# Sigmoid gates and SiLU by a hyperbolic tangent, and a bias added on VectorE, in an mLSTM and two-MLP kernel

## The chip, the cores and the metric

One core of one Trainium2 chip. The time is microseconds of device time of one launch; lower is better. Several runs of a kernel are taken and the median is compared. One execution was profiled: the trace and its page are of that one.

## What is computed

An mLSTM (matrix memory with exponential gates) over 2 sequences of 768 steps with 8 heads of width 40, then two MLPs of 320 to 2048 to 320 on its 1536 output rows, the first with SiLU, the second with Mish. All in fp32:

```
m_new = max(f[t] + m, i[t])
C = exp(f[t] + m - m_new) * C + exp(i[t] - m_new) * outer(v[t], k[t]);  n likewise with k[t]
y[t] = sigmoid(o[t]) * (C q[t]) / max(|n q[t]|, 1)
h = x @ w_in;  g = h * sigmoid(h)          (layer 1: SiLU)
out = g @ w_out                            (layer 2: g = h * tanh(softplus(h)))
```

## The kernel before, in words

**Attention.** The 768 steps are cut into 6 chunks of 128 (`attention(c)`, with both sequences of a chunk together). Inside a chunk the recurrence is written as a product: scores k.q (L748) times a weight tile e (L757, into `pt`), times v (L762, into `a`), plus the state carried from the chunk before (L781, from chunk 1 on). The tile e of 128x512 holds the exponentials for four heads side by side; a chunk has four such tiles (u = 0 to 3). In chunks 0 and 1 the exponent is spread by TensorE into PSUM (L692, L694, tile `fp`), and ScalarE takes four exponentials of 128x128, one a head, since each head has its own bias per partition, a column of `bT` (L704). In chunks 2 to 5 the exponent comes by DMA and is masked by GpSimd (L717), then exponentiated in place (L730, also one head at a time).

**Gates.** The output gates of a chunk are loaded into `y1[c]`, 128x640, and `sigm` takes their sigmoid in place (L649): chunks 0 and 1 behind the last exponential of chunk 0's attention, chunks 2 to 5 behind that of chunk 2. Then GpSimd divides them by the denominator (L816), and VectorE multiplies them into the attention's output x (L819). x is transposed on TensorE (L897) and split into a high part `xh` (L907) and a low part `xl` (L910).

**Weights.** Each weight block f (16 per layer) arrives as 64-bit floats (`wr`, three buffers), is turned into fp32 by two ScalarE passes (L471, L463) and one VectorE join (L477), and split into `wh` (ScalarE, L503) and `wl` (GpSimd, L497; VectorE, L501). A buffer of `wr` is free for the next load once its join is done. All loads are issued from SP's queue, in one order.

**MLP.** A block of the first GEMM makes a PSUM tile h of 128x512 (two weight blocks by 256 rows of x, L930, 16 matmuls). ScalarE takes Silu into `g` (L964), GpSimd rounds g to `gh` (L955), VectorE forms `gl` = g - gh (L957), and the second GEMM (L947 to L949) multiplies both parts with the output weights; it runs two blocks behind the first. For chunks 0 and 1 the first layer is run in two halves (five block pairs, then three), and `store_y` keeps the first half's sum in y (`first`, L983) and adds the second half's (`more`, L987); other chunks use `first` alone. Layer 2 uses Mish (L973, L974).

**What sets the order.** Nothing is written in the order in which it runs. Every operation is handed to a planner with its engine, an estimated cost in us, the tiles that it reads and writes, and the name of the activation table that it needs. The planner simulates the engines, adds 1.28 us on ScalarE where the table changes and prefers not to change it, improves the order by 1500 random draws with a fixed seed, and then emits each engine's instructions in the order found. A changed cost, engine or table name so gives a new order for all engines. Each engine runs its own list in order. Up to 20 matmuls on a dummy tile (L445) fill TensorE while it has nothing else at the start.

Of the kernel before, what the change touches and what calls it, by code (L numbers as in the profile page):

```python
# [13 lines left out]
AF = mybir.ActivationFunctionType  # L14
ALU = mybir.AluOpType
# [23 lines left out]
class Plan:  # L39
# [13 lines left out]
    def buf(self, pool, shape, dtype, tag, bufs=1, name=None):  # L53
        b = Buf(pool, shape, dtype, tag, bufs, name or tag)
        ring = self.rings.setdefault((id(pool), tag), [])
        b.before = ring[-bufs] if len(ring) >= bufs else None
        b.prev = ring[-1] if ring else None
        ring.append(b)
        return b
# [310 lines left out]
def kernel(  # L370
# [17 lines left out]
    DM = out.shape[1]  # L388
# [10 lines left out]
    op, buf = plan.op, plan.buf  # L399
    pe, act, dve, pool = nc.tensor, nc.scalar, nc.vector, nc.gpsimd  # L400
# [21 lines left out]
    def mk4():  # L422
        return mk.t.unsqueeze(1).to_broadcast([128, 4, 128])
# [102 lines left out]
    bT = buf(sb, [128, NCH, 16], F32, "bT")  # L526
# [112 lines left out]
    last_e = [None]  # L639
# [3 lines left out]
    y1 = [buf(sb, [128, B, DM], F32, f"y{c}") for c in range(NCH)]  # L643
# [2 lines left out]
    last = NCH - 1  # L646

    def sigm(c, after):
        return op("ACT", 0.74, lambda: act.activation(out=y1[c].t, in_=y1[c].t, func=AF.Sigmoid),  # L649
           w=[y1[c]], table="sig", after=after)  # L650

    def load_o(c, after=()):
        dma(y1[c], None, lambda: y1[c].t, lambda: og[c], 128 * B * DM * 4, after=after)
# [1 line left out]
    def attention(c):  # L655
        A = "attn"
        hurry = HURRY0 if c == 0 else HURRY
        g0 = gate_of[c]

        kq = buf(sb, [104, 2048], F32, "kq")  # L660
        for e in range(2):
            r = slice(64 * e, 64 * e + D)
# [17 lines left out]
        for u in range(4):  # L680

            if c >= PEBC and ((c - PEBC) * 4 + u) % 7 < 3:
                e = buf(sb, [128, 512], F32, "ga", bufs=3)
            else:
                e = buf(sb, [128, 512], F32, "e", bufs=EB)
            es.append(e)
            if c < PEBC:

                fp = buf(ps, [128, 512], F32, ("h", "h", "o0", "h")[u], bufs=(2, 2, 1, 2)[u])

                def spread(u=u, fp=fp):
                    pe.matmul(out=fp.t, lhsT=idb.t, rhs=mk4(), start=True, stop=False)  # L692
                    for i in range(4):
                        pe.matmul(  # L694
                            out=fp.t[:, i * 128:(i + 1) * 128],
                            lhsT=ct.t[:, u * 4 + i:u * 4 + i + 1].to_broadcast([128, 128]),
                            rhs=gc.t[:, c * 128:(c + 1) * 128], start=False, stop=(i == 3),
                        )

                def weight(u=u, e=e, fp=fp):  # L700
                    for i in range(4):
                        k = slice(i * 128, (i + 1) * 128)
                        j = u * 4 + i
                        act.activation(out=e.t[:, k], in_=fp.t[:, k], func=AF.Exp, bias=bT.t[:, c, j:j + 1])  # L704

                op("PE", 1.09, spread, r=[idb, mk, ct, (gc, c)], w=[fp], hurry=hurry, duty=0.59)
                last_e[0] = op("ACT", 1.14, weight, r=[(bT, g0), fp], w=[e], table="exp", hurry=hurry,
                               after=sig if c == 0 else ())
                continue

            def row(u=u):
                return gd.t[4 * u:4 * u + 4, :].rearrange("h t -> (h t)").unsqueeze(0).to_broadcast([128, 512])


            def cut(e=e):
                ev = e.t.rearrange("p (h t) -> p h t", h=4)
                pool.affine_select(  # L717
                    out=ev, in_=ev, pattern=[[0, 4], [1, 128]], base=0, channel_multiplier=-1,
                    compare_op=ALU.is_ge, fill=-1e30,
                )  # L720

            dma(e, gd, lambda e=e: e.t, row, 128 * 2048, hurry=hurry)
            op("POOL", 0.59, cut, w=[e], hurry=hurry, grain=0.7)
# [8 lines left out]
        for us in EXPS[c] if c >= PEBC else []:  # L732
            last_e[0] = op("ACT", 1.28 * len(us), lambda us=us: exps(us), r=[(bT, g0)], w=[es[u] for u in us],
                           table="exp", hurry=hurry)
        for i in SIGS.get(c, ()):
            sigm(i, [last_e[0]])
        xs = []
        for b in range(2):
# [12 lines left out]
            for hf in range(2):  # L751
                u = 2 * b + hf
# [49 lines left out]
            else:  # L802
# [3 lines left out]
               r=[nsrc], w=[dn], hurry=hurry)  # L806
# [153 lines left out]
    def silu(hp):  # L960
        g = buf(sb, [128, 512], F32, "g", bufs=2)
        gh = buf(sb, [128, 512], F32R, "gh", bufs=3)
        gl = buf(sb, [128, 512], F32R, "gl", bufs=3)
        op("ACT", 0.6, lambda: act.activation(out=g.t, in_=hp.t, func=AF.Silu), r=[hp], w=[g], table="silu")  # L964
        parts(g, gh, gl)
        return gh, gl

# [11 lines left out]
    def store_y(c, b, po, part):  # L979
        y = y1[c]  # L980

        def first():
            act.copy(out=y.t[:, b, :], in_=po.t[:, 0:DM])  # L983


        def more():
            dve.tensor_tensor(out=y.t[:, b, :], in0=y.t[:, b, :], in1=po.t[:, 0:DM], op=ALU.add)  # L987

        if part == 2:
            op("DVE", 0.49, more, r=[po], w=[(y, b)])  # L990
        else:
            op("ACT", 0.43, first, r=[po], w=[(y, b)])
# [42 lines left out]
    sig = [sigm(c, ()) for c in SIGS.get(-1, ())]  # L1035
# [173 lines left out]
```

## Time and profile before

| | |
|---|---|
| median of 3 runs | 450.71 us (449.8 to 451.85) |
| profiled execution | span 447.9 us from the first to the last instruction; no other time of it is shown |
| mean granted TensorE clock | 0.973 of full speed (2.4 GHz) |
| busy: TensorE, VectorE, ScalarE, GpSimd | 435.0, 196.2, 249.4, 145.1 us |
| ScalarE table loads | 34, of 1.28 us each |

A busy share is of the whole span. PE is TensorE's matmuls and PEld its weight loads, which run beside them; DVE is VectorE, ACT ScalarE, POOL GpSimd, SP the queue from which transfers are issued. L964 is line 964 of the kernel. An engine's idle time matters only where that engine, or one that waits for it, sets the end.

### The profile page before, as it was taken

Reading aid. Unit: us, or ns where it says so; the run is one execution under the profiler, and the core shown is the slowest. Engines: PE = TensorE matmul, PEld = TensorE weight load, DVE = VectorE, ACT = ScalarE, POOL = GpSimd, SP = SyncE. Lnnn points to the kernel's source line nnn. Section 1 sums busy time; section 2 is a strip of 40 time slices with the busy share of each in tenths; the row PEclk is TensorE's granted clock in tenths of the full one; section 3 lists DMA queues with packets and bytes.
Section 4 is the critical chain, followed back from the end, with each engine's and each line's share of the span. In section 5 each row is a group of like instructions: output and inputs, shape, how many; then the busy total and the mean of one; then the engine's idle time right before and its main releaser. Section 6 shows DMA issues by size and latency. Waiting matters only on the chain.

```text
span 447.9 us, 8297 instructions
## 1 busy us (share of the span) xinstructions
PE 435.0 (97%) x3366; PEld 424.6 (95%) x3366; DVE 196.2 (44%) x340; ACT 249.4 (56%) x441; POOL 145.1 (32%) x208
## 2 busy tenths in 40 slices
PE   7978989999999999999999999999999999999997
PEld 4858889999999999999999999999999999999996
DVE  4486587644774555664442644322131221221111
ACT  1898667799989888873124447433343333333331
POOL 1777686862361434122113996300000000000000
PEclk9956969999999999999999999999999999999999
DMA  7869979152475767865000453100000000000000
GB/s 223 301 225 268 324 241 318 67 166 71 112 249 185 291 213 277 279 205 201 3 1 1 131 156 103 34 31 0 2 31 0 1 31 0 31 1 0 31 2 29
DMA packets 16785, 54.18 MB, mean 121 GB/s; under 512 B 2003, under 2 KB 3731, under 8 KB 16267
## 3 DMA queue, kind: packets, MB, share of 16 engines
q1 hardware_dynamic: 16747, 53.65, 36.5%
q8 instruction: 26, 0.43, 0.4%
q14 instruction: 12, 0.10, 0.1%
HBM read 45.88 MB, written 7.77 MB: 120 GB/s over the span
## 4 chain that ended last, share of the span: by engine, by line
PE 89%; POOL 4%; ACT 3%; DMA 2%; issue 1%; DVE 1%; POOLq 0%; ACTq 0%
PE h L930 29%; PE o L947 12%; PE o L949 12%; PE o L948 12%; PE s L930 10%; PE a L762 4%; PE s L748 2%; POOL wl L497 2%; PE a L897 2%; DMA wr<-w 2%; PE o L445 1%; PE a L781 1%; PE a L846 1%; ACT e L704 1%; PE h L694 1%
## 5 line engine op out<-in xcount | busy, mean ns | idle before, releaser
L947 PE MATMUL o<-wh,gh 128*128 128x320 f32 x384 | 121.1, 315 | 0.0
L949 PE MATMUL o<-wh,gl 128*128 128x320 f32 x384 | 119.1, 310 | 0.4 <-DVE gl L957 0.4
L948 PE MATMUL o<-wl,gh 128*128 128x320 f32 x384 | 118.4, 308 | 0.0
L930 PE MATMUL h<-xh,wh 128*128 128x256 f32 x432 | 111.0, 286 | 0.0
L930 PE MATMUL h<-xl,wh 128*128 128x256 f32 x432 | 109.0, 281 | 0.0
L975 DVE TENSOR_TENSOR gl<-e,gh 128x512 fp32r<-128x512 f32 x48 | 33.8, 703 | 126.6 <-ACT e L974 126.6
L930 PEld LDWEIGHTS h<-xh,wh 128*128 128x128 f32 x432 | 82.5, 191 | 0.6 <-issue 0.2
L930 PEld LDWEIGHTS h<-xl,wh 128*128 128x128 f32 x432 | 82.3, 190 | 0.0
L949 PEld LDWEIGHTS o<-wh,gl 128*128 128x128 f32 x384 | 72.1, 188 | 0.7 <-DVE gl L957 0.7
L947 PEld LDWEIGHTS o<-wh,gh 128*128 128x128 f32 x384 | 72.3, 188 | 0.5
L948 PEld LDWEIGHTS o<-wl,gh 128*128 128x128 f32 x384 | 72.3, 188 | 0.0
L497 POOL TENSOR_TENSOR wl<-wt,wh 128x192 fp32r<-128x192 f32 x96 | 64.7, 704 | 15.9 <-ACT wh L503 13.4
L957 DVE TENSOR_TENSOR gl<-g,gh 128x512 fp32r<-128x512 f32 x48 | 40.6, 851 | 43.9 <-POOL gh L955 43.7
L930 PE MATMUL h<-xh,wl 128*128 128x256 f32 x288 | 58.0, 283 | 0.0
L955 POOL TENSOR_SCALAR gh<-g 128x512 fp32r<-128x512 f32 x48 | 32.3, 674 | 77.2 <-ACT g L964 74.9
L964 ACT ACTIVATE g<-h 128x512 f32<-128x512 f32 x48 | 28.5, 598 | 41.4 <-PE h L930 40.9
L930 PEld LDWEIGHTS h<-xh,wl 128*128 128x128 f32 x288 | 44.3, 190 | 0.0
L973 ACT ACTIVATE gh<-h 128x512 fp32r<-128x512 f32 x24 | 14.5, 602 | 50.5 <-PE h L930 50.4
L973 ACT ACTIVATE gh<-s 128x512 fp32r<-128x512 f32 x24 | 14.4, 601 | 49.5 <-PE s L930 49.5
L930 PE MATMUL s<-xh,wh 128*128 128x256 f32 x144 | 36.4, 282 | 0.0
L930 PE MATMUL s<-xl,wh 128*128 128x256 f32 x144 | 36.0, 279 | 0.0
L477 DVE SCALAR_TENSOR_TENSOR wt<-wt,wr 128x704 int32<-128x704 int32 x32 | 31.8, 997 | 5.7 <-ACT wt L463 5.1
(101 smaller groups left out, 621.0 us busy)
## 6 DMA issues: line engine op xcount, KB each, us to landing
wr<-w SPq DMA_DIRECT2D x32, 704.0 KB, 6.4
wd<-wt SPq DMA_DIRECT2D x16, 352.0 KB, 5.3
wt<-wd SPq DMA_DIRECT2D x16, 352.0 KB, 3.1
vk<-vk SPq DMA_DIRECT2D x6, 729.0 KB, 4.0
kq<-qk SPq DMA_DIRECT2D x12, 320.0 KB
e<-gd SPq DMA_DIRECT2D x8, 256.0 KB, 5.9
ga<-gd SPq DMA_DIRECT2D x8, 256.0 KB, 3.3
y<-og SPq DMA_DIRECT2D x6, 320.0 KB, 11.3
```

What stands on the lines that cost most here:

```text
L477: dve.scalar_tensor_tensor(out=ti, in0=ti, scalar=3, in1=r.t[:, :, 0], op0=ALU.logical_shift_left, op1=ALU.bitwise_or)
L497: pool.tensor_tensor(out=wl.t[:, k], in0=t.t[:, k], in1=wh.t[:, k].bitcast(F32), op=ALU.subtract)
L762: pe.matmul(out=pa.t[:, h * V:(h + 1) * V], lhsT=pt.t[:, i * 128:(i + 1) * 128], rhs=vb.t[:, b, h * V:(h + 1) * V], start=True, stop=True,)
L930: pe.matmul(out=hp.t[:, f % 2 * 256:(f % 2 + 1) * 256], lhsT=w.t[:, k], rhs=xx.t[:, i, :], start=(n == 0), stop=(n == len(terms) - 1),)
L947: pe.matmul(out=o, lhsT=gh.t[:, ts], rhs=wh.t[:, O], start=(first and f == 0), stop=False)
L948: pe.matmul(out=o, lhsT=gh.t[:, ts], rhs=wl.t[:, O], start=False, stop=False)
L949: pe.matmul(out=o, lhsT=gl.t[:, ts], rhs=wh.t[:, O], start=False, stop=(end and f == 1))
L955: op("POOL", 0.63, lambda: pool.tensor_scalar(out=gh.t, in0=g.t, scalar1=1.0, scalar2=1.0, op0=ALU.mult, op1=ALU.mult), r=[g], w=[gh])
L957: op("DVE", 0.75, lambda: dve.tensor_tensor(out=gl.t, in0=g.t, in1=gh.t.bitcast(F32), op=ALU.subtract), r=[g, gh], w=[gl], grain=1.0)
L964: op("ACT", 0.6, lambda: act.activation(out=g.t, in_=hp.t, func=AF.Silu), r=[hp], w=[g], table="silu")
L973: op("ACT", 0.6, lambda: act.activation(out=gh.t, in_=hp.t, func=AF.Mish), r=[hp], w=[gh], table="mish")
L975: op("DVE", 0.7, lambda: dve.tensor_tensor(out=gl.t, in0=g.t, in1=gh.t.bitcast(F32), op=ALU.subtract), r=[g, gh], w=[gl])
```

## The change

The gates' sigmoid becomes tanh(o/2) on ScalarE and 0.5 z + 0.5 on GpSimd, in place. SiLU becomes tanh(h/2) on ScalarE and (z + 1) h on VectorE, which is twice SiLU; the factor of two is taken out where the first layer's output is copied or added to y (times 0.5). Both tanh are named to the planner as needing the exponential's table. In chunks 0 and 1 VectorE adds the bias of four heads to the spread exponents, from PSUM into e, and ScalarE takes one exponential of 128x512 in place.

```diff
--- before.py
+++ after.py
@@ -646,8 +646,11 @@
     last = NCH - 1
 
     def sigm(c, after):
-        return op("ACT", 0.74, lambda: act.activation(out=y1[c].t, in_=y1[c].t, func=AF.Sigmoid),
-           w=[y1[c]], table="sig", after=after)
+        o = op("ACT", 0.74, lambda: act.activation(out=y1[c].t, in_=y1[c].t, func=AF.Tanh, scale=0.5),
+           w=[y1[c]], table="exp", after=after)
+        op("POOL", 0.85, lambda: pool.tensor_scalar(
+            out=y1[c].t, in0=y1[c].t, scalar1=0.5, scalar2=0.5, op0=ALU.mult, op1=ALU.add), w=[y1[c]])
+        return o
 
     def load_o(c, after=()):
         dma(y1[c], None, lambda: y1[c].t, lambda: og[c], 128 * B * DM * 4, after=after)
@@ -697,15 +700,16 @@
                             rhs=gc.t[:, c * 128:(c + 1) * 128], start=False, stop=(i == 3),
                         )
 
-                def weight(u=u, e=e, fp=fp):
-                    for i in range(4):
-                        k = slice(i * 128, (i + 1) * 128)
-                        j = u * 4 + i
-                        act.activation(out=e.t[:, k], in_=fp.t[:, k], func=AF.Exp, bias=bT.t[:, c, j:j + 1])
+                def shift(u=u, e=e, fp=fp):
+                    dve.tensor_tensor(
+                        out=e.t.rearrange("p (h t) -> p h t", h=4), in0=fp.t.rearrange("p (h t) -> p h t", h=4),
+                        in1=bT.t[:, c, 4 * u:4 * u + 4].unsqueeze(2).to_broadcast([128, 4, 128]), op=ALU.add,
+                    )
 
                 op("PE", 1.09, spread, r=[idb, mk, ct, (gc, c)], w=[fp], hurry=hurry, duty=0.59)
-                last_e[0] = op("ACT", 1.14, weight, r=[(bT, g0), fp], w=[e], table="exp", hurry=hurry,
-                               after=sig if c == 0 else ())
+                op("DVE", 0.7, shift, r=[(bT, g0), fp], w=[e], hurry=hurry)
+                last_e[0] = op("ACT", 0.6, lambda e=e: act.activation(out=e.t, in_=e.t, func=AF.Exp),
+                               w=[e], table="exp", hurry=hurry, after=sig if c == 0 else ())
                 continue
 
             def row(u=u):
@@ -961,7 +965,9 @@
         g = buf(sb, [128, 512], F32, "g", bufs=2)
         gh = buf(sb, [128, 512], F32R, "gh", bufs=3)
         gl = buf(sb, [128, 512], F32R, "gl", bufs=3)
-        op("ACT", 0.6, lambda: act.activation(out=g.t, in_=hp.t, func=AF.Silu), r=[hp], w=[g], table="silu")
+        op("ACT", 0.6, lambda: act.activation(out=g.t, in_=hp.t, func=AF.Tanh, scale=0.5), r=[hp], w=[g], table="exp")
+        op("DVE", 0.7, lambda: dve.scalar_tensor_tensor(
+            out=g.t, in0=g.t, scalar=1.0, in1=hp.t, op0=ALU.add, op1=ALU.mult), r=[hp], w=[g])
         parts(g, gh, gl)
         return gh, gl
 
@@ -980,11 +986,13 @@
         y = y1[c]
 
         def first():
-            act.copy(out=y.t[:, b, :], in_=po.t[:, 0:DM])
+            act.mul(out=y.t[:, b, :], in_=po.t[:, 0:DM], mul=0.5)
 
 
         def more():
-            dve.tensor_tensor(out=y.t[:, b, :], in0=y.t[:, b, :], in1=po.t[:, 0:DM], op=ALU.add)
+            dve.scalar_tensor_tensor(
+                out=y.t[:, b, :], in0=po.t[:, 0:DM], scalar=0.5, in1=y.t[:, b, :], op0=ALU.mult, op1=ALU.add
+            )
 
         if part == 2:
             op("DVE", 0.49, more, r=[po], w=[(y, b)])
```

## Rows read from the trace of the kernel before

**Rows 1.** The page's first part: busy us (share of the span) and instructions by engine
```profile
PE 435.0 (97%) x3366; PEld 424.6 (95%) x3366; DVE 196.2 (44%) x340; ACT 249.4 (56%) x441; POOL 145.1 (32%) x208
```

**Rows 2.** Stretches of the span: length, each engine's busy us (instructions), clock, DMA
```profile
core 0: us, PE busy (x) PEld busy (x) DVE busy (x) ACT busy (x) POOL busy (x), PEclk, DMA share, GB/s
22.50:24.00 1.50, 0.26 (x3) 0.14 (x2) 0.31 (x1) 1.50 (x3) 0.88 (x2) 0.98 0.16 30
24.00:36.00 12.00, 8.97 (x43) 7.37 (x44) 11.09 (x21) 11.11 (x24) 7.31 (x11) 0.50 0.72 242
...
36.00:41.00 5.00, 5.00 (x31) 4.55 (x30) 4.31 (x7) 4.54 (x7) 4.68 (x6) 0.50 0.96 268
41.00:52.00 11.00, 10.57 (x81) 10.31 (x81) 5.49 (x8) 8.91 (x13) 8.85 (x13) 1.00 1.01 317
...
120.00:130.00 10.00, 10.00 (x91) 9.68 (x90) 8.70 (x13) 8.30 (x12) 6.24 (x7) 1.00 0.62 188
...
300.00:440.00 140.00, 140.00 (x1082) 139.95 (x1081) 30.44 (x50) 47.53 (x93) 0.00 (x0) 1.00 0.04 13
```

**Rows 3.** The chain that ended last: start us, us, what
```profile
17.73 1.28 ACT L649
...
19.77 1.28 ACT L704
21.06 1.14 ACT e L704 x4
22.20 0.73 ACT wr L471
...
24.50 0.69 DVE pt L757
...
131.99 1.89 PE h L930 x16
135.63 1.89 PE h L930 x16
```

**Rows 4.** Timeline of TensorE around 23 us: start, us, what [idle before it]
```profile
20.89 1.88 PE L762 MATMUL a<-vk,pt 128*128 128x41 f32 x16
25.23 3.64 PE L762 MATMUL a<-vk,pt 128*128 128x41 f32 x16 [2.47 <-DVE pt L757]
```

**Rows 5.** Timeline of ScalarE, VectorE and SP's queue before 43 us
```profile
16.57 1.14 ACT L704 ACTIVATE e<-h,bT 128x128 f32<-128x128 f32 x4
...
23.69 0.89 DVE L477 SCALAR_TENSOR_TENSOR wt<-wt,wr 128x704 int32<-128x704 int32 x1 [3.08 <-ACT wt L463]
...
24.61 4.10 SPq L403 DMA_DIRECT2D wr<-w  x3
...
39.63 1.28 ACT L649 ACT_TABLE_LOAD   x1
...
41.68 1.28 ACT L964 ACT_TABLE_LOAD   x1
```

**Rows 6.** Waits of TensorE: who waited for whom, us in total, times, longest
```profile
PE o L949 <- DVE gl L957: 0.4, 1, 0.4
```

**Rows 7.** Instruction groups (ScalarE within 70 to 266 us): busy, mean ns | idle before
```profile
L964 ACT ACTIVATE g<-h 128x512 f32<-128x512 f32 x44 | 26.1, 598 | 39.0 <-PE h L930 38.6
L964 ACT ACT_TABLE_LOAD x14 | 18.0, 1283 | 3.4 <-PE h L930 3.2
...
L730 ACT ACT_TABLE_LOAD x10 | 12.8, 1283 | 0.2
...
L649 ACT ACT_TABLE_LOAD x4 | 5.1, 1283 | 0.1
...
L955 POOL TENSOR_SCALAR gh<-g 128x512 fp32r<-128x512 f32 x48 | 32.3, 674 | 77.2 <-ACT g L964 74.9 <-DVE xl L910 2.3
...
L555 POOL TENSOR_SCALAR ga<-ga 80x512 f32<-80x512 f32 x1 | 1.5, 1492 | 0.1
```

**Rows 8.** Two lines of VectorE: duration ns min/median/max, first and last start us
```profile
L957 DVE TENSOR_TENSOR gl<-g,gh x48: 676/693/1203, 44.7 to 262.7; 128x512 fp32r<-128x512 f32 x48
...
L757 DVE TENSOR_TENSOR pt<-e,s x16: 677/681/689, 14.3 to 210.4; 128x512 f32<-128x512 f32 x16
```

## The prediction

> **What bounds the kernel now.** I read the page's busy shares first, to see which engine to follow: TensorE is busy for 97% of the 447.9 us span, ScalarE for 56%, VectorE for 44%, GpSimd for 32% [rows 1]. An average over unlike stages says little, so I cut the span into stretches. From 70 us to 440 us TensorE is never idle at a granted clock of 1.00; the stretches 120 to 130 and 300 to 440 stand for all of them [rows 2]. There ScalarE cannot be what sets the end. Before 70 us it is different: TensorE works 0.26 of 1.5 us, then 8.97 of 12, and its granted clock is 0.50 from 24 to 41 us, 1.2 GHz instead of 2.4 [rows 2]. So the question is only what the change does to the first 70 us, and whether it spoils the full stretch behind them.
>
> The chain of waits names the cause of the first hole. ScalarE loads the sigmoid table at 17.73, gates one tile, loads the exponential's table again at 19.77, does four exponentials, and only then, from 22.20, turns to the first weight block [rows 3]. VectorE's join of that block starts at 23.69 after 3.08 us of waiting for ScalarE, and the product pt, which needs nothing of the weights, stands behind it in VectorE's order and starts at 24.50 [rows 3, 5]. TensorE had finished the previous group of 16 products at 20.89 + 1.88 = 22.77 and starts the next at 25.23: a hole of 2.46 us. In front of the hole 16 matmuls took 1.88 us, behind it 16 of the same took 3.64, since the clock had fallen [rows 4]. Everything of chunk 0, its outputs x and the first GEMM, follows behind that.
>
> **The change, part by part.**
> *Table loads.* 28 loads, 18.0 + 12.8 + 5.1 = 35.9 us of ScalarE, lie between 70 and 266 us [rows 7]. They lie beside a TensorE that is full: worth 0. Four count: the two at 17.73 and 19.77, and the two around the second gate tile at 39.63 and 41.68, each 1.28 us [rows 3, 5].
> *Exponentials of chunks 0 and 1.* Four of 128x128 cost 1.14 us of the engine (the chain's row at 21.06); one over 512 columns should cost what the other 512-column activation costs, 0.60 us [rows 3, 7]. Two such groups, at 16.57 and 21.06, stand ahead of the first weight block [rows 3, 5]: 2 x 0.54 = 1.08. VectorE gets eight additions that read PSUM and write 512 columns; nearest row pt, 0.68 us [rows 8], 5.4 us in all. From 20.6 to 23.69 VectorE only waits, so I cost those that fall there at 0; without that cover each costs 0.68 (rival below). One group's latency grows by 0.68 + 0.60 - 1.14 = 0.14 us, hidden by TensorE's products before it.
> *First hole.* ScalarE reaches the weights 2 x 1.28 + 1.08 = 3.6 us earlier, so the join is over before pt can start. pt then waits only for its buffer, which the products from 20.89 release, so I expect the 2.46 us hole closed. If TensorE does not pause there, the next group also runs at the full clock: 3.64 - 1.88 = 1.76. Sum 4.2 us for chunk 0's chain. The weights move too: SP issues the next weight loads at 24.61, right behind the join [rows 5], and these issues come up to 3.6 us earlier. The DMA engines can carry that: unused share 0.84 x 1.5 + 0.28 x 12 = 4.6 us before 36 us [rows 2]. From 36 to 52 us they are full (0.96 and 1.01), so what lands there moves by no more than 3.6. Bounds of this term: 0 (the hole opens elsewhere) to 4.2; I take **3.6**, because the full DMA stretch is nearest to what decides the time up to 52 us.
> *Second pair of loads.* Without them the first SiLU tile starts up to 2 x 1.28 = 2.57 us earlier. TensorE's wait for that tile's low part gl is 0.4 us in all [rows 6]: **0.4**, bounds 0 and 2.57.
> *SiLU in two steps.* Tanh costs what Silu did (0.60), and VectorE adds 48 passes over a PSUM tile at 0.68, 32.6 us in all. For the first tile the pass is hidden by the 2.57 just freed. From 70 us on each tile has cover: the second GEMM runs two blocks behind, and a block lasts 135.63 - 131.99 = 3.64 us of TensorE [rows 3], against 0.68. The tightest stretch is 120 to 130 us, VectorE busy 8.70 of 10 [rows 2]; two or three more passes fill it. If that cover is gone, three late tiles cost 3 x 0.68 = 2.0. I take 0 and keep 2.0 for the range.
> *Gates.* Six GpSimd passes over 640 columns. The nearest row, the same form with two constants over 512, is 0.67, so 0.67 x 640/512 = 0.84; the other row, one constant over 80x512, is 1.49, so at most 1.9 [rows 7]. I take 0.84. Behind such a pass stand the weights' low parts and the key scaling in GpSimd's order, and VectorE's x waits for them through the gate. One falls before 36 us, where GpSimd is busy 7.31 of 12 [rows 2]: 0. The second tile's gate is not needed until chunk 1, so 0; placed ahead of SiLU's rounding in the backlog of 36 to 41 us (4.68 of 5) it costs 0.84 to 1.9.
> *Halving at the first layer's end* replaces instructions one for one, with the same operands: 0. No DMA is added or moved past another by hand; the planner draws its whole order anew, whose effect no row bounds other than the ends below.
> Contention: gl, with two SBUF inputs, varies from 676 to 1203 ns; pt, with one input in PSUM, stays within 677 to 689 [rows 8]. The new VectorE passes are like pt, hence 0.68. The Trainium skill ("GPSIMD Engine Reference", section Specifications) says that GpSimd shares its SBUF interfaces with VectorE and collides with VectorE instructions that have two SBUF inputs. The rows on gl and pt agree; by that rule the two early gate passes could stretch a join or gl by 1203 - 676 = 527 ns each, and the sum would be about 1.1 us smaller, 447.8.
>
> **Sum.** 3.6 + 0.4 = 4.0 us off a span of 447.9 gives 443.9. The median of the runs shown, 450.7, lies 2.8 above that span; the profiled execution has no other time shown, so I leave the 2.8 as it is: **446.7 us**.
>
> **Rivals.**
> *A, the forecast* (443 to 448.4).
> *B, hidden anyway.* The hole closes but chunk 1's input waits for the same transfers, so TensorE starves later instead. For it: DMA share 0.96 and 1.01 from 36 to 52 us. Against: the unused 4.6 us before. Only the 0.4 is left: 450.3.
> *C, VectorE becomes the bound of the start.* It is busy 11.09 of 12 us from 24 to 36 and 4.31 of 5 behind [rows 2]. If the four additions of chunk 1 stand there, among joins and pt, they put back the chain they were to free: 4 x 0.68 = 2.7, with nothing gained, 453.4 us. It decides once more than the free time, 0.91 + 1.19 (VectorE works 0.31 of the 1.5 us ahead) = 2.1 us, has to be found there, that is from the fourth addition on. Against: ScalarE freed early pulls the joins out of this stretch.
> *D, the clock does not fall.* If the closed hole keeps TensorE at 2.4 GHz through 24 to 41 us, its 8.97 + 5.00 us of work there shrink by half, 7.0, of which 1.76 is counted: 446.7 - 5.2 = 441.5. Against: it also pauses for the transposes, 3 of 12 us.
> *E, the change does not do what it says.* If Tanh is not in the exponential's table the loads stay, and the first SiLU tile pays 0.68 and chunk 1 the 0.14: 451.5. The trace before runs no Tanh and cannot tell. The Trainium skill ("ScalarE: Activation LUTs", section on table sets) lists tanh as a member of exp_and_others; no run here shows it.
>
> **How the numbers follow.** About 0.5% (2.25 us) is what a measurement of this kernel can tell from no change. A 0.47 and D 0.13 are faster: 0.60. B 0.20 and E 0.03 are within: 0.23. C is slower: 0.17. The likeliest is A: 446.7. The low end is D's 441.5 less 0.5 of the 0.4's upper bound, 441.0; the high end is C's 453.4. Outside lie a D that also gains behind 52 us, and a C with the late tiles' 2.0 on top: 0.2 together.
>
> **What would show it.** Right: one table load before the SiLU stage and one for Mish; four rows of 512-column exponentials per chunk at 0.60; the additions at 0.68; no hole near 22.8 us; the first weight issues behind the first three at about 21; TensorE full from about 66 us. Wrong: VectorE idle less than 0.9 us between 22 and 36 with pt waiting for its queue (C); the same wait moved to a DMA of vk or wr (B); TensorE idle behind 70 us, released by gl (the cover of the late tiles is gone).

## The result, and the profile after

The changed kernel takes **452.94 us** (median of 20 runs, 452.06 to 453.70); the kernel before took 450.07 beside it (20 runs, 447.55 to 454.48). The ratio is 1.0063, 95% interval 1.0046 to 1.0080: 0.6% slower. The forecast was 446.7, faster. The value lies inside the range, but on the side of the chance of 0.17.

The profiled execution has a span of 451.4 us, against 447.9 before, and a time of 453.1, so 1.7 us lie around the span. (The forecast added 2.8. The other 1.1 would mean that the execution profiled before was quicker than its median.) 3.5 us of span have to be found.

First the page's row of busy time by engine.

```profile
PE 435.3 (96%) x3366; PEld 424.1 (94%) x3366; DVE 229.9 (51%) x396; ACT 204.9 (45%) x385; POOL 153.5 (34%) x214
```

Then the groups of instructions that the change made or left (line, engine, operation, tiles, count; busy us, mean ns of one; idle time before them and what ended it):

```profile
L968 ACT ACTIVATE g<-h 128x512 f32<-128x512 f32 x48 | 28.7, 597 | 55.5 <-PE h L934 52.2 <-DVE gl L961 3.2
...
L711 ACT ACTIVATE e<-e 128x512 f32<-128x512 f32 x8 | 4.8, 626 | 1.9 <-DVE e L704 1.9
L607 ACT ACT_TABLE_LOAD x1 | 1.3, 1283 | 0.8 <-PEq L1207 0.8
L979 ACT ACT_TABLE_LOAD x1 | 1.3, 1283 | 0.0
...
L969 DVE SCALAR_TENSOR_TENSOR g<-g,h 128x512 f32<-128x512 f32 x48 | 32.8, 684 | 26.8 <-ACT g L968 26.5
...
L704 DVE TENSOR_TENSOR e<-h,bT 128x512 f32<-128x512 f32 x6 | 4.0, 681 | 1.0 <-PE h L697 1.0
...
L651 POOL TENSOR_SCALAR y<-y 128x640 f32<-128x640 f32 x6 | 5.6, 925 | 4.3 <-ACT y L649 4.2
```

The change does what it says [rows 1, 7]. Of 34 table loads two are left, ScalarE works 44.5 us less, VectorE 33.7 us more, GpSimd 8.4 more, and TensorE's busy time is the same. One exponential over 512 columns took 0.626 us, SiLU's tanh 0.597, the addition 0.681, the SiLU pass 0.684, the gate pass 0.925 on average.

Now the start. This is the timeline of after from 20 to 38 us, all engines (start us, us, engine, line, what, and in brackets the idle time before it and who ended it); it answers to [rows 3 to 5].

```profile
20.91 0.74 ACT L649 ACTIVATE y<-y 128x640 f32<-128x640 f32 x1 [3.11 <-DMA y<-og]
...
22.60 0.83 ACT L471 ACTIVATE wr<-wr 128x704 int32<-128x704 uint16 x1
...
24.18 1.82 DVE L477 SCALAR_TENSOR_TENSOR wt<-wt,wr 128x704 int32<-128x704 int32 x1 [4.17 <-ACT wt L463]
25.92 0.68 DVE L761 TENSOR_TENSOR pt<-e,s 128x512 f32<-128x512 f32 x1
...
26.65 3.60 PE L766 MATMUL a<-vk,pt 128*128 128x41 f32 x16 [3.44 <-DVE pt L761]
...
28.48 7.01 POOL L497 TENSOR_TENSOR wl<-wt,wh 128x192 fp32r<-128x192 f32 x9
35.46 0.71 POOL L820 TENSOR_TENSOR y<-y,dn 128x320 f32<-128x320 f32 x1
...
36.20 0.49 DVE L823 TENSOR_TENSOR x<-a,y 128x320 f32<-128x320 f32 x1 [2.81 <-POOL y L820]
...
36.84 0.66 PE L901 MATMUL a<-ct,x 128*128 128x128 f32 x2 [3.74 <-DVE x L823]
```

Read it from the top. The table loads in front of the first weight block are gone, and ScalarE still reaches that block (L471) only at 22.60; it was 22.20 before [rows 3]. It sits idle for 3.11 us in front of the tanh of the *second* gate tile, whose transfer, issued at 7.27 us, has not landed. The whole old chain then follows: join at 24.18, pt behind it, and TensorE's hole is 3.44 us instead of 2.47 [rows 4]. The join adds to it: it takes 1.82 us, where the one before took 0.89 [rows 5], beside two GpSimd passes (at 23.97 and, the gate pass of the second tile, at 25.33). A second wait is new: GpSimd makes nine low parts of weights, 7.01 us, before it divides a gate by the denominator, so x is late and TensorE waits 3.74 us. The chain that ended last has that transfer as one of its longest pieces (start us, us, what):

```profile
7.27 13.62 DMA y<-og
```

The waits of TensorE repeat those for x and pt (3.7 and 3.4 us) and show two smaller ones (who waited for whom, us in total, times, longest):

```profile
PE o L953 <- DVE gl L961: 1.0, 3, 0.6
...
PE o L951 <- POOL gh L959: 0.6, 1, 0.6
```

Last, stretches of after (length; busy us and instructions of TensorE's matmuls, its weight loads, VectorE, ScalarE, GpSimd; granted clock, DMA):

```profile
0.00:75.00 75.00, 62.92 (x451) 54.58 (x452) 54.75 (x106) 40.71 (x66) 48.06 (x69) 0.89 0.78 254
...
24.00:36.00 12.00, 6.40 (x35) 5.55 (x35) 8.71 (x16) 9.66 (x16) 10.70 (x14) 0.63 0.70 228
...
27.00:45.00 18.00, 13.54 (x71) 12.11 (x71) 14.40 (x29) 13.20 (x22) 14.39 (x19) 0.53 0.83 281
...
58.00:65.00 7.00, 6.71 (x62) 6.20 (x60) 6.80 (x13) 3.20 (x5) 6.95 (x10) 1.00 0.67 202
...
95.00:100.00 5.00, 4.21 (x30) 3.86 (x30) 3.82 (x7) 3.25 (x10) 5.00 (x8) 1.00 0.63 247
...
300.00:440.00 140.00, 140.00 (x1073) 139.95 (x1072) 30.23 (x50) 48.02 (x93) 0.00 (x0) 1.00 0.04 13
```

and three of these stretches in the kernel before:

```profile
0.00:75.00 75.00, 65.35 (x447) 57.40 (x448) 49.68 (x98) 53.03 (x98) 48.23 (x71) 0.84 0.83 269
...
58.00:65.00 7.00, 7.00 (x43) 6.78 (x40) 5.37 (x13) 3.79 (x7) 6.24 (x9) 0.51 0.70 225
...
95.00:100.00 5.00, 5.00 (x50) 4.76 (x50) 1.16 (x2) 4.95 (x10) 1.63 (x4) 1.00 0.29 68
```

Three things stand there (the row of 24 to 36 us is for a rival, below; the rows of 0 to 75 us are read after the next table). The clock falls once more in the start, for about as long as before (0.53 over 18 us), but a second fall, at 58 to 65 us in the kernel before, is gone: 62 matmuls instead of 43 in those 7 us. At 95 to 100 us TensorE is idle for 0.79 us, where it was never idle. And in the last 140 us, with TensorE busy for all of them at clock 1.00 in both kernels, it finished **1073 matmuls instead of 1082** [rows 2].

That last line can't be seen in a busy share, so I made an account by work done. For each stretch I took its length less the matmuls that start in it, each at the spacing that its form has in the full stretch of the kernel before (0.118 us in the first GEMM, 0.147 in the second, and so on). The work so priced is 410.8 us in every kernel here; what is left over is lost time:

| lost us in | 0–75 | 75–110 | 110–200 | 200–266 | 266–300 | 300–440 | rest | sum |
|---|---|---|---|---|---|---|---|---|
| before | 29.7 | 0.5 | 1.9 | 0.8 | 0.3 | 0.4 | 3.5 | 37.1 |
| after | 29.1 | 1.7 | 2.7 | 1.6 | 0.4 | 1.6 | 3.5 | 40.6 |

So of the 3.5 us, the start gave back 0.6 where about 4 was forecast, 1.2 was lost at 75 to 110 us, and 2.9 behind 110 us, in stretches where TensorE looks full in both.

The 0.6 is the difference of two larger things. TensorE is idle for 12.08 of the first 75 us in after and for 9.65 before: the waits cost 2.4 us more. Against that, the mean granted clock of these 75 us is 0.89 instead of 0.84, because the second fall did not come. That fall cost the kernel before about 3.4 us (an estimate from its row: TensorE busy for all of the 7.00 us at 0.51, so about half of them lost). Without this gain the start would have come out about 2.8 us slower than before.

### The profile page after: what moved, and what is told of

Same layout as the page of the kernel before. It is cut to its first block, busy times and chain, and to the rows that moved or that the text cites. A ratio compares the mean times of both kernels' runs of the same rounds, so it can differ in the third digit from the quotient of the medians.

```text
span 451.4 us, 8352 instructions
## 1 busy us (share of the span) xinstructions
PE 435.3 (96%) x3366; PEld 424.1 (94%) x3366; DVE 229.9 (51%) x396; ACT 204.9 (45%) x385; POOL 153.5 (34%) x214
## 4 chain that ended last, share of the span: by engine, by line
PE 80%; POOL 8%; DMA 4%; DVE 2%; issue 2%; ACT 2%; SPq 0%; POOLq 0%; ACTq 0%
PE h L934 26%; PE o L951 12%; PE o L953 11%; PE o L952 11%; PE s L934 10%; POOL wl L497 6%; PE a L766 3%; DMA y<-og 3%; PE s L752 2%; PE a L901 2%; PE a L785 1%; DMA ga<-gf 1%; PE a L850 1%; POOL gh L959 1%; DVE gl L961 1%
## 5 line engine op out<-in xcount | busy, mean ns | idle before, releaser
L934 PE MATMUL h<-xh,wh 128*128 128x256 f32 x432 | 112.6, 289 | 0.0
L934 PE MATMUL h<-xl,wh 128*128 128x256 f32 x432 | 110.9, 286 | 0.7 <-DVE xl L914 0.7
L959 POOL TENSOR_SCALAR gh<-g 128x512 fp32r<-128x512 f32 x48 | 33.9, 708 | 71.2 <-DVE g L969 62.1
L969 DVE SCALAR_TENSOR_TENSOR g<-g,h 128x512 f32<-128x512 f32 x48 | 32.8, 684 | 26.8 <-ACT g L968 26.5
```

Source lines behind the costliest of these rows:

```text
L934: pe.matmul(out=hp.t[:, f % 2 * 256:(f % 2 + 1) * 256], lhsT=w.t[:, k], rhs=xx.t[:, i, :], start=(n == 0), stop=(n == len(terms) - 1),)
L959: op("POOL", 0.63, lambda: pool.tensor_scalar(out=gh.t, in0=g.t, scalar1=1.0, scalar2=1.0, op0=ALU.mult, op1=ALU.mult), r=[g], w=[gh])
L969: op("DVE", 0.7, lambda: dve.scalar_tensor_tensor(out=g.t, in0=g.t, scalar=1.0, in1=hp.t, op0=ALU.add, op1=ALU.mult), r=[hp], w=[g])
```

## The experiments

Two theories stood at first: that the change is a gain in itself and the planner's new order gives it back, and that the passes added on VectorE and GpSimd cost the time in any order. A third came up for the last 140 us: that the tiles' places in SBUF slow the matmuls. Medians of the kernel before differ between the chips that the runs were taken on (449.66 to 451.21 us), so across chips I compare ratios to the kernel before and the account of lost time, not medians. Added lines shift the line numbers of each experiment by a few.

### The change in the order of the kernel before

To take the planner out, the order that it found for the kernel before was written down and used as a list, with the added operations put in where they fall due. q1 has the whole change, q2 the tanh half alone, q3 the bias half alone.

```diff
     def issue(self):
+        for n in ORDER:
+            self.ops[n].fn()
+        self.ops = []
+        return
```

> The whole change, but each engine runs its list in the order of the kernel before, with the 62 added operations put in where their inputs are due. Theory 1 (the change itself is a small gain; the planner's new order costs the 2.9 us): at or below the kernel before, 446 to 450 us, centre 447.5. Theory 2 (the added VectorE and GpSimd passes cost it in whatever order): 452 to 455 us, as slow as the changed kernel or slower.

> Only the hyperbolic tangent half of the change (gates, SiLU, the halving), exponentials as before, order of the kernel before. Theory 1: the loads at 17.7, 19.8, 39.6 and 41.7 us are gone and nothing else moves: 447 to 449.5 us. Theory 2: 48 SiLU passes and six gate passes cost more than the loads gave: 451 to 454 us.

> Only the bias half of the change (eight additions on VectorE, one exponential for four heads in chunks 0 and 1), sigmoid and Silu and their loads as before, order of the kernel before. Theory 1: ScalarE saves 2 x 0.54 us ahead of the first weight block: 449 to 450.1 us. Theory 2: VectorE, busy from 24 to 41 us, gets up to 2.7 us more: 451 to 453 us.

Measured: q1 456.00 us, ratio 1.0123 [1.0075, 1.0171]; q2 455.78, 1.0113 [1.0064, 1.0162]; q3 452.12, 1.0035 [1.0006, 1.0064]. q1 and q2 are slower than even the second theory expected (455 and 454 us at most); q3 lies inside its range. So the theory that the change is a gain in itself fell in this form: in an order made for the other instructions it costs 1.2%. But the traces show two different things. q2, timeline of ScalarE (L475 is the first weight block):

```profile
19.28 1.14 ACT L711 ACTIVATE e<-h,bT 128x128 f32<-128x128 f32 x4 [0.54 <-PE h L701]
20.30 0.86 ACT L475 ACTIVATE wr<-wr 128x704 int32<-128x704 uint16 x1
```

q2, waits of TensorE:

```profile
PE o L954 <- POOL gh L962: 1.3, 1, 1.3
...
PE a L769 <- DVE pt L764: 1.2, 3, 0.5
```

q2, one stretch:

```profile
90.00:100.00 10.00, 8.16 (x48) 7.64 (x47) 6.62 (x8) 6.40 (x19) 6.62 (x10) 0.83 0.45 163
```

The weights start at 20.30 instead of 22.20, and the hole in front of pt has shrunk from 2.47 to 0.5 at the longest: the first step of the prediction, as it was worked out. It is lost at 90 to 100 us, where GpSimd's gh comes 1.28 us late; TensorE is then busy for 8.16 of 10 us and its granted clock is 0.83 on average. The account has 4.4 us lost in 75 to 110, against 0.5 before, and the start not shorter (30.3), since the freed time opens waits for tw and x: TensorE is idle for 9.94 of the first 75 us, against 9.65 before, and the clock's mean is 0.84 in both. Closing the hole alone so brought nothing.

In q1 the bias half undoes even the first step. Timeline of ScalarE and VectorE:

```profile
21.77 0.63 ACT L715 ACTIVATE e<-e 128x512 f32<-128x512 f32 x1 [2.26 <-DVE e L708]
...
18.41 2.44 DVE L563 TENSOR_TENSOR_SCAN gc<-ga 80x128 f32<-80x128 f32 x4 [0.27 <-POOL ga L559]
...
21.00 0.67 DVE L708 TENSOR_TENSOR e<-h,bT 128x512 f32<-128x512 f32 x1
```

The addition that ScalarE waits for stands behind four scans in VectorE's list, and the 2.26 us that ScalarE waits are most of the 2 x 1.28 of the loads that went. That addition was costed at 0 in the prediction because VectorE "only waits" from 20.6 on; it was due before that. In q3 ScalarE waits 0.83 us for an addition and then still loads the table; TensorE's longest wait for pt is 3.3 us, in an execution 2.8 us above q3's median.

### The new order, mended

p1, p2 and p3 each make one move in the order of the changed kernel, p4 all three.

```diff
 p1, ScalarE and POOL: the second gate tile's tanh and its pass
-    before chunk 0's exponentials
+    behind the passes of the fifth weight block
 p2, POOL: chunk 0's second division
-    behind the low parts of two weight blocks
+    ahead of them
 p3, SP: the load of sel
-    ahead of gi, ct and gf (the gates)
+    behind them
```

> The changed kernel in its own order with three moves: the second gate tile's tangent and its GpSimd pass go behind the fifth weight block's ScalarE passes; the division of chunk 0's second gate goes ahead of the second and third weight blocks' low parts on GpSimd; the load of sel goes behind the two gate loads on SP. Theory 1: the 3.1 us in which ScalarE waits for that tile's transfer, most of the 3.7 us in which TensorE waits for x, and the 2.6 us later start of the gates go: 446 to 449.5 us. Theory 2: those waits only change places, 451.5 to 454 us.

> The changed kernel with one move: the second gate tile's tangent and its GpSimd pass behind the fifth weight block's ScalarE passes. If ScalarE's 3.1 us wait for that tile's transfer is what spoils the start: the first weight block starts by 20.7 us instead of 22.6, TensorE's 3.4 us hole shrinks to about 1.5, 451 to 452 us. Rival (the weights or the products were not waiting for ScalarE): 452.5 to 453.5 us with the hole unchanged.

> The changed kernel with one move: the division of chunk 0's second gate ahead of the second and third weight blocks' low parts on GpSimd. If those low parts are what x waits for: TensorE's 3.7 us wait for x at 36.8 falls below 1 us and 450 to 451.5 us. Rival (x is early but the first GEMM then waits for the low parts that were put back): the wait moves to the first GEMM and 452.5 to 453.5 us.

> The changed kernel with one move: SP issues the load of sel behind the two gate loads, as in the kernel before. If the 2.6 us later start of the gates costs the start: 450.5 to 452 us. Rival (chunk 0's scores wait for their own transfer, and start at 13.0 us in both): 452.5 to 453.5 us.

Measured: p4 450.88 us, 1.0014 [0.9982, 1.0047]; p1 452.17, 1.0063 [1.0044, 1.0082]; p2 451.69, 1.0045 [1.0025, 1.0065]; p3 452.30, 1.0037 [1.0007, 1.0068]. The profiled starts lost 27.7 (p1), 28.0 (p2), 28.0 (p3) and 26.4 us (p4), against 29.1 in after. Each of the four lies between the range that it was expected in and that of its rival. p1's timelines of ScalarE, VectorE, GpSimd and TensorE:

```profile
20.01 0.83 ACT L475 ACTIVATE wr<-wr 128x704 int32<-128x704 uint16 x1
...
25.45 4.67 DVE L481 SCALAR_TENSOR_TENSOR wt<-wt,wr 128x704 int32<-128x704 int32 x1
...
26.59 3.98 POOL L501 TENSOR_TENSOR wl<-wt,wh 128x192 fp32r<-128x192 f32 x6
...
23.38 1.08 PE L770 MATMUL a<-vk,pt 128*128 128x41 f32 x8 [0.81 <-DVE pt L765]
25.58 1.08 PE L770 MATMUL a<-vk,pt 128*128 128x41 f32 x8 [1.12 <-DVE pt L765]
30.66 0.66 PE L905 MATMUL a<-ct,x 128*128 128x128 f32 x2 [1.98 <-DVE x L827]
35.09 0.66 PE L905 MATMUL a<-ct,x 128*128 128x128 f32 x2 [3.56 <-DVE x L827]
```

With the transfer out of the way the weights start 2.6 us earlier (20.01) and the hole of 3.44 falls to 0.81 + 1.12, but the waits for x grow from 3.74 to 1.98 + 3.56: most of the time only moves. What x stands behind on VectorE is one join that took 4.67 us; the join before it took 0.88. GpSimd runs its passes beside it without a break, six low parts among them, and in p4 the join at that place took 3.02 us. But in after two joins beside low parts took 0.86 us each (at 32.53 and 40.80), so what stretched this one is open. p2 does the reverse; its waits of TensorE:

```profile
PE a L770 <- DVE pt L765: 3.4, 1, 3.4
...
PE o L955 <- POOL gh L963: 1.5, 1, 1.5
PE a L905 <- DVE x L827: 1.0, 1, 1.0
```

x is no longer late, pt is still, and gh is new. p3 starts the gates earlier and leaves both waits. The three moves together bring the start 3.3 us under the kernel before (26.4 against 29.7), a number near the 4.0 that the prediction summed, but not by its mechanism: TensorE is idle for 9.08 of the first 75 us, only 0.6 less than before, and the rest of the gain is the clock, 0.89 on average as in after. Against after (12.08 idle, the same clock) the moves gave back 3.0 us of waiting. Yet p4 is no faster than the kernel before: by the account it loses 1.9 us at 75 to 110 (0.5 before) and 9.6 behind 110 (6.9 before). So the order of the start was one cause of the loss against the forecast, and there had to be another, behind it.

### Where the matmuls slow down

In this code a tile gets its place in SBUF when the emitted order first touches it, so a new order also means new places. In the kernel before, the tiles wh (the weights' high parts) come first and the two tiles dn of 128x8 fp32 later; in after dn comes first, and wh starts 2 x 32 = 64 bytes further, while xh, xl and the weights' low parts wl keep their places. gh, gl, g and a few others move too. a1 is after with wh touched ahead of dn, a2 the kernel before with dn touched ahead of wh, a3 is p4 with wh ahead; a6 is the kernel before with 64 bytes inserted ahead of wh, so that it and all tiles behind it move together.

```diff
 a1 (a2: o.n == 176 and "dn"; a3: as a1, in the list of p4)
         for o in best:
+            if o.n == 79:
+                [r for (_, t), r in self.rings.items() if t == "wh"][0][0].t
             o.fn()
 a6
+    PAD.append(buf(sb, [128, 16], F32, "pad"))
...
         for o in best:
+            if o.n == 176:
+                PAD[0].t
             o.fn()
```

> The changed kernel, same instructions in the same order; only the high weights wh get the place in SBUF that they had before (92512 instead of 92576, ahead of the two dn tiles instead of behind them). Theory 3 (the first GEMM's matmuls run 2 to 3 ns slower each because wh lies 64 bytes further): from the first s tile of layer 2 to the end 179.4 us instead of 180.8, about 5 us less in the stretch from 110 to 440, 447 to 449.5 us in all. Rival (the slower matmuls come from the added VectorE and GpSimd passes or from the order): 452 to 454 us, and 180.8 us to the end.

> The kernel before, same instructions in the same order; only the two dn tiles of 32 bytes are placed ahead of wh, so that wh lies at 92576 as in the changed kernel. Theory 3: slower by 3.5 to 5 us, 453.5 to 455 us, and 180.8 us from the first s tile of layer 2 to the end. Rival: no difference, 449.5 to 450.5 us, 179.4 us.

> The changed kernel with the three moves in its order and wh at its old place. Theory 3, if the moves and the place add up: 450.9 - 4.5 = 446.4, 445 to 448 us, clearly faster than the kernel before. Rival: 450 to 452 us.

> The kernel before with 64 unused bytes ahead of wh, so that wh, wl, xh and xl all lie 64 bytes further and their distances stay. If what matters is where wh lies against the other operands: no difference, 179.4 us to the end. If what matters is wh's own place: 180.8 us to the end and 453 to 455 us.

Measured: a1 451.32 us, 0.9990 [0.9972, 1.0007]; a2 453.24, 1.0043 [1.0014, 1.0071]; a3 449.46, 0.9956 [0.9935, 0.9978]; a6 450.85, 0.9984 [0.9954, 1.0013]. a2 changes nothing but places, and costs 0.4%. a6 moves wh and everything behind it by the same 64 bytes, and costs nothing: so, for this one distance, it is where operands lie to each other, not the place itself. a3, the mended order with wh ahead, is already faster than the kernel before. The third theory had the direction but too much: a1 and a3 lie between its range and the rival's, a2 just under its range.

a7 gives the changed kernel all the places of the kernel before, and a8 does so for p4:

```diff
     def issue(self):
+        for tag in PLACES.split():
+            next(r for (_, t), r in self.rings.items() if t == tag)[0].t
```

> The changed kernel, same instructions in the same order, every SBUF tile at the place that it had before. If places explain all of the slower matmuls behind 110 us: 179.4 us from the first s tile of layer 2 to the end, 110 to 440 us as dense as before, about 1.5 us less than with wh alone moved, 448.5 to 450 us. Rival (the rest comes from the added VectorE passes): 180.0 us to the end, no gain over wh alone, 450.5 to 452 us.

> The changed kernel with the three moves in its order and every SBUF tile at its old place. If moves and places add up: 447 to 448.5 us, ratio to the kernel before 0.990 to 0.995. If they don't: as with wh alone, 449 to 450.5.

Measured: a7 450.47 us, 1.0018 [1.0002, 1.0033]; a8 448.64, 0.9974 [0.9957, 0.9991]. Against the same orders with their own places (1.0063 and 1.0014) that is 0.45% and 0.40% of 450 us, 2.0 and 1.8 us. Both lie between the two ranges that were expected. By these ratios wh alone (a1, 0.73% under after; a3, 0.58% under p4) gave more than all places together, while the rows below and the account (from 9.8 to 7.1 us behind 110 us in a7) say the reverse. a1 and a3 ran on another chip, where the kernel before was slower, 451.21 against 449.66 us. So the effect is shown, and its size is known only as 0.4 to 0.7% of the time. The rows of one kind of matmul of layer 2, by tile (duration ns as min/median/max, then the first and the last start in us), in the kernel before:

```profile
L930 PE MATMUL s<-xh,wh x144: 276/279/365, 268.5 to 438.8; 128*128 128x256 f32 x144
```

after:

```profile
L934 PE MATMUL s<-xh,wh x144: 280/283/365, 270.6 to 442.3; 128*128 128x256 f32 x144
```

a2, the kernel before with dn first:

```profile
L932 PE MATMUL s<-xh,wh x144: 274/283/365, 271.1 to 442.1; 128*128 128x256 f32 x144
```

a7, the changed kernel in the old places:

```profile
L936 PE MATMUL s<-xh,wh x144: 276/279/365, 268.9 to 439.2; 128*128 128x256 f32 x144
```

From first to last these take 170.3, 171.7, 171.0 and 170.3 us. The work between is the same and TensorE waits for nothing in it; a few nanoseconds a matmul are all of the difference. In the same view the matmuls of xl with wh went from a median of 279 ns before to 283 after as well, those of xh with wl, which did not move, from 282 to 283. a7 begins layer 2 at 268.9 and after at 270.6: before layer 2, too, most of the 2.1 us by which after was late (270.6 less 268.5) went with the places. By these rows moving wh alone is about half of it (171.0 in a2, and 1076 matmuls in the last 140 us of a1, against 1073 and 1082); which other tile makes the rest was not tried.

### Is it this one order?

The planner's search is random with a fixed start, so one order could be bad or good luck. s2 takes both kernels from another start (both in the old places, as a7).

```diff
-SEED = 1
+SEED = 2
```

> The kernel before, every SBUF tile at its place, the planner's random search started from 2 instead of 1: another order of the same instructions. If the order that the search happens to give is worth more than the change: it differs from the kernel before by 1 us or more, 451 to 455 us. If orders are worth little: within 1 us of it.

> The changed kernel, every SBUF tile at the places of before, the search started from 2. If the order decides: 1 us or more away from the 450.5 us that the changed kernel has at these places with the search started from 1, and on average over both starts no slower than the unchanged instructions. Rival (the change itself costs): again above the kernel before, and above the unchanged instructions searched from 2.

Measured: the kernel before 448.67 us, 0.9979 [0.9945, 1.0014]; the changed one 450.71, 1.0009 [0.9978, 1.0039]. The second order of the changed kernel has the same two waits, pt 3.9 and x 3.8 us in all. So the waits are not those of one draw alone. The unchanged kernel came out faster from the other start, where the expectation had a different order slower; the interval takes in 1. Against the kernel before as it stands, the changed one is level within 0.2% in both orders (1.0018, 1.0009); against the kernel before from this other start it is 0.45% behind (450.71 to 448.67), with both intervals taking in 1. Two draws are few.

### The best version

p5 is a8 with three kinds of further moves: the two pt of chunk 0 ahead of the weight joins, x right behind its division on GpSimd, and the low parts of one weight block behind a gh. The expectation puts the last one at 96 us; in the trace it acted near 80 us.

```diff
 VectorE, chunk 0
-join, pt, join, pt
+pt, join, pt, join
-scan, join, x
+x, scan, join
 GpSimd, near 80 us
-wl, gh
+gh, wl
```

> The changed kernel with the three moves, all tiles at the places of before, and three more moves: chunk 0's third and fourth products pt ahead of the weight joins that stand before them on VectorE; chunk 0's second x right behind its gate's division, ahead of a gate scan and a join; the low parts of one later weight block behind the two roundings gh that wait for them at 96 us on GpSimd. If the waits left (1.9 us for pt, 2.6 us for x, 1.3 us for gh) were the order's alone: 446 to 448 us. Rival (VectorE is full there and something else comes late): 448.2 to 449.5 us, as without them.

Measured: 447.57 us (447.05 to 448.65), ratio 0.9947 [0.9922, 0.9972], faster than both kernels. Its waits of TensorE:

```profile
PE a L907 <- DVE x L829: 3.8, 2, 2.0
...
PE a L907 <- DVE tw L900: 2.1, 1, 2.1
PE o L957 <- POOL gh L965: 1.2, 1, 1.2
PE o L959 <- DVE gl L967: 1.1, 3, 0.6
...
PE a L772 <- DVE pt L767: 0.5, 1, 0.5
```

The wait for pt is down to 0.5. What is left is x and tw in the start, and gl and gh. The join that took 3.03 us in a8 (at 26.17) takes 0.85 (at 25.97). The account over all versions that matter, with TensorE's idle time and mean granted clock in the first 75 us:

| lost us in | 0–75 | 75–110 | behind 110 | sum | ratio | idle, 0–75 | clock, 0–75 |
|---|---|---|---|---|---|---|---|
| before | 29.7 | 0.5 | 6.9 | 37.1 | 1 | 9.7 | 0.84 |
| after | 29.1 | 1.7 | 9.8 | 40.6 | 1.0063 | 12.1 | 0.89 |
| a7: after, old places | 28.6 | 1.7 | 7.1 | 37.5 | 1.0018 | 10.5 | 0.86 |
| p4: order mended | 26.4 | 1.9 | 9.6 | 37.9 | 1.0014 | 9.1 | 0.89 |
| a8: both | 27.1 | 2.0 | 7.3 | 36.5 | 0.9974 | 9.5 | 0.89 |
| p5: six moves, old places | 26.2 | 1.8 | 6.8 | 34.8 | 0.9947 | 11.9 | 0.91 |
| q1: change in the old order | 32.5 | 2.9 | 8.1 | 43.5 | 1.0123 | 9.9 | 0.82 |

So in the start even p5 does not make TensorE wait less than the kernel before (11.9 against 9.7 us idle); it gains by the clock. And the kernel before was given no such moves: another order of its unchanged instructions took 448.67 us on the same chip. p5 shows what the changed kernel can reach, not that the change is worth it.

## Why the prediction was wrong

**Right.** The table loads are gone: 34 became 2, and rival E is out. The Trainium skill ("ScalarE: Activation LUTs", section "Table sets: the hidden batching unit") puts tanh into the exponential's set, and the trace agrees. The prices held: exponential 0.626 for 0.60, addition 0.681 and SiLU pass 0.684 for 0.68, gate pass 0.925 on average for 0.84. The 28 loads behind 70 us brought nothing that the account shows. The chain of the first hole was read rightly: q2 takes the loads away in the old order, and the hole goes.

**The step that failed** is the term of 3.6 us for the first hole, and behind it this sentence: "the planner draws its whole order anew, whose effect no row bounds other than the ends below". It was written down and then costed at 0. Two things came through it (the first and the last below), and one more term at 0 held only in the planner's order.

- *"so I expect the 2.46 us hole closed."* The hole had two conditions, no table loads and nothing else of ScalarE's list in front of the weights that comes late. The second was taken for granted: "The second tile's gate is not needed until chunk 1, so 0". Before, that tile was gated at about 41 us [rows 5]. Without a table to keep apart, the planner put its tanh in front of chunk 0's exponentials, and the wait for its transfer (3.11 us) stood where the loads (2 x 1.28) had been. The hole became 3.44 instead of 0, and behind it x became late by 3.74 behind nine low parts on GpSimd. And where the hole did close, in q2, TensorE was idle as long as before (9.94 and 9.65 us): the next waits, for tw and x, took the gain. The term of 3.6 measured 0.6 in the account, and even that is less than what the clock's second fall gave back by not coming, about 3.4.
- *"so I cost those that fall there at 0"*, of the additions. In the planner's new order they were early enough; in the old order (q1) one of them stood behind four scans and held ScalarE for 2.26 us. That is rival C's mechanism, VectorE's queue, though at another place and in another kernel. In after itself VectorE was idle for 3.29 of the 12 us from 24 to 36 (busy 8.71 us in the row above), where C wanted less than 0.9: C did not happen.
- *The slower matmuls* were in no step and no rival. Nothing in the trace before could show them; that a new order is also a new allocation could have been read in the code. It is the largest piece of the 2.9: about 2.0 us between after and a7 by their ratios.

That p4 and p5 end 3.3 and 3.5 us under the kernel before in the start, near the 4.0 of the sum, is luck: the sum was of waits and loads that go, and these are mostly of the clock (TensorE is idle for 0.6 us less in p4 and 2.2 us more in p5 than before).

**Mis-sized.** "three late tiles cost 3 x 0.68 = 2.0. I take 0": the cover behind 70 us did fail at one place, 95 to 100 us, released by gl as the list of signs had it. The account has 1.2 us. The timeline of GpSimd and VectorE in after points to a cause, which is not the SiLU passes alone:

```profile
93.50 4.57 POOL L497 TENSOR_TENSOR wl<-wt,wh 128x192 fp32r<-128x192 f32 x6
98.04 1.20 POOL L959 TENSOR_SCALAR gh<-g 128x512 fp32r<-128x512 f32 x2
...
98.69 2.29 DVE L961 TENSOR_TENSOR gl<-g,gh 128x512 fp32r<-128x512 f32 x2 [1.08 <-POOL gh L959]
```

Six low parts stand ahead of two gh, and the two gl, which need gh, take 1.15 us each behind them. That the order on GpSimd is the cause is read from these lines and was not tried: p5 moved low parts near 80 us, not these six, and 1.8 us stay lost there. The "second pair of loads" (0.4) brought nothing: the wait for gl at 45 us was replaced by one of 0.64 for gh at 47 and one of 0.16 for gl.

**The rivals.** B had the right kind of end, a transfer in the place of the wait removed, but named vk and wr; it was og. That its 450.3 is where a7 lies (450.47), the changed kernel with the places of before, is chance. D did not happen: 0.53 from 27 to 45 us. What the clock did give was somewhere else, at 58 to 65 us, a stretch that the prediction's rows left out although its fall stood in the trace before. The mean clock of that stretch is 0.51 before and 0.56 to 0.63 in q1 to q3, which keep the old order, and 1.00 in after, p1 to p5, a7 and a8; why, the runs don't show.

The collisions that the prediction weighed and left out of its sum show in single joins, not on average: gl took 840 ns on average after and 851 before, but the join in front of pt in after took 0.93 us more than before, and the one in p1 3.8 us more than its neighbour. The Trainium skill ("GPSIMD Engine Reference", section Specifications) says that GpSimd shares its SBUF interfaces with VectorE and collides with VectorE instructions that have two SBUF inputs, as a join has. The trace agrees in that GpSimd works beside both of these joins (in after, the gate pass among its passes); that two other joins beside low parts took 0.86 us shows that it does not always cost.

So, of the 0.63%: at equal places the change is about a draw (1.0018). There the new order's waits (10.5 us idle in the first 75, against 9.7, and 1.2 us more lost at 75 to 110) eat what the clock gives (0.86 against 0.84). The places add the other 0.45%, by these ratios.

## What to carry to other kernels

Where a planner or an allocator reacts to a change, two kernels differ in more than the diff: compare them once at fixed places and once with the order's waits taken out, before you judge the change. When a fixed cost in front of an in-order engine goes, ask of each later entry in its list whether its transfer has landed by then; the nearest one that has not can be the new wait. Where a hole closes, look at TensorE's idle time over the whole stretch and at its granted clock, each by itself: a gain in one can hide a loss in the other. A TensorE that is busy for 100% of a stretch at full clock is not at a fixed rate: count the matmuls in the stretch.

## What the hardware showed that I had not expected

Matmuls of the same shape and clock took 279 or 283 ns (118 or about 120 ns from start to start), by where their weights' tile lay relative to the other operands. A distance of 64 bytes was enough (a2: 1.0043 with nothing but places changed), and moving wh and all tiles behind it together by 64 bytes did nothing (a6: 0.9984 [0.9954, 1.0013], 1082 matmuls in 140 us as before). Which operands disturb each other, and through what, the runs don't show.

A join of 128x704 on VectorE took 0.88 us in one place and 4.67 us in another of the same run (p1), beside GpSimd's passes.

A transfer of 320 KB issued at 7.27 us took 13.62 us to land. The page of that trace gives 4.7 us for its kind, but min, median and max are the same there: it is one landing of six. The page of the kernel before gives 11.3 us for one. So such a figure says little of the start unless one knows when its transfer was issued.
